# Windowed attention and a routed expert layer on one core: logits in transposed groups, opening products, routing in three steps, scatters without order

## The chip, the core and the metric

The kernel runs on one core of a Trainium2 chip. TensorE (PE) multiplies, VectorE (DVE) and ScalarE (ACT) work on tiles, GpSimd (POOL) builds constants and issues the indirect DMAs, SyncE (SP) and ACT issue the plain ones. All five have queues of their own and wait for each other by semaphores. The metric is the device time of one launch in microseconds: the median of three runs. Beside it there is one profiled execution, from which every duration in this document is read.

## What is computed

Two stages follow each other.

The first is attention in chunks, for 4 batches, 8 heads, 768 tokens and 64 dimensions a head. A chunk of 32 queries sees 8 memory keys, 16 keys to its left, its own 32 and 8 to its right. The outputs of the 8 heads side by side are a token's row x of 512 numbers.

```
scores = scale * q_c @ concat(mem_k, k_ctx).T
a = softmax(scores)
out[:, :, c_start:c_end] = a @ concat(mem_v, v_ctx)
```

The second is a layer of 8 experts, each token using one of them. A token takes the expert with the largest logit (the first of equals), or, if its local gate is at least 0.5, the expert of the token before it in its batch. Its output is weighted with the softmax of the logits at the chosen expert.

```
fresh_e = int(np.argmax(logits[b, s]))
e = fresh_e if s == 0 or local_gate[b, s] < 0.5 else prev_e
h = np.maximum(x[b, s] @ w1[e], 0.0)
out[b, s] = p[e] * (h @ w2[e])
```

All data are float32. A product in float32 shows as two passes in the trace, each with a weight load, so that the counts of products there are twice those of the code. A transpose on TensorE shows as one.

## The kernel before

**Attention.** The 3072 tokens are 32 blocks of 96 tokens, 8 to a batch. `load` (L103) fetches a block's q, k and v, three blocks ahead; q and k are issued by SP, v by ACT. `scores` (L176) makes 8 products, keys by queries, for the two halves of the dimensions' partitions alternately, and ACT turns them into weights with three exps (L188), with the mask as bias. `values` (L191) makes 8 products into one PSUM tile `o_ps`; v carries a column of ones, so that the sum of the weights comes out as the 65th column, and DVE takes its reciprocal (L198) and multiplies (L200) into the token rows `x`. `logits` (L237) turns the block's 96x512 rows by four transposes (L240), ACT copies them to SBUF (L242), and four accumulated products (L245) take the turned tokens as weights and the 9 gate columns (8 experts and the local gate) as the moving operand. DVE copies the 96x9 result (L246).

**Routing.** After the eighth block of a batch `route` (L248) runs once. DVE finds the largest logit and the index of the first, and codes place and expert in one number for tokens that choose anew. Eight products (L273) lay these codes out along one row, four to a PSUM tile, and a running maximum (L277) carries the last choice forward. The expert is cut out of the code by two passes (L279, L280), a one-hot row for each expert is made (L282), and a running sum (L284), carried over batches in `count`, gives each token its rank in its expert. Eight products (L291) bring the row numbers back to the tokens. DVE works out the softmax weight of the chosen expert (L297 to L311), and POOL writes the rows of the eight blocks to `x_dram` in eight indirect scatters (L314), 4096 rows of room for each expert.

**Experts.** When all rows are written, `experts` (L354) works out a table of tiles of 128 rows of one expert each. For every tile, POOL gathers the rows (L435), SP fetches the expert's two weight matrices of 2 MB each (L439, L441; four buffers), PE transposes the rows (L447) and makes 32 products (L460), ACT applies ReLU (L462), PE makes 8 products with 512 moving columns (L465), ACT applies the token's weight (L467) and POOL scatters the output (L468). 24 tiles always run; up to seven more run under conditions.

**Order.** The kernel is written as dataflow on tiles, and a planner at build time sets the order of each engine's instructions and places the semaphores. It is free to move work that doesn't depend on each other: the profile shows the transposes of one block behind the scores of the next. Buffers are reused in a ring for each name. PSUM has two buffers for scores, one tile for `o_ps`, one for transposed blocks (`tps`, L100) and one that logits and the two products of routing share (`xps`, L101). The planner orders two writes to one tensor: each scatter to `x_dram` waits for the one before it, since it can't know that their rows differ.

At the end of attention the kernel counts the softmax sums that lie in a safe range (L342 to L350); only if one doesn't, the whole computation runs again in a shifted form (L82). With the inputs here it doesn't.

Of the kernel before, what the change touches and what calls it, by code (L numbers as in the profile page):

```python
# [8 lines left out]
F32 = mybir.dt.float32  # L9
# [15 lines left out]
MASKED = -1e30  # L25

# [11 lines left out]
SHIFT = 12  # L38
FAR = 4096
WBUF = 4  # L40
# [12 lines left out]
def kernel(  # L53
# [22 lines left out]
    attention(tc, q, k, v, w_gate, w_local, x_dram, ident, count, kept_i)  # L76
    experts(tc, x_dram, out, ident, count, w1, w2)
# [3 lines left out]
    with tc.If(kept < NT * H):  # L81
        attention(tc, q, k, v, w_gate, w_local, x_dram, ident, count, None)  # L82
        experts(tc, x_dram, out, ident, count, w1, w2)
# [3 lines left out]
def attention(ctx, tc, q, k, v, w_gate, w_local, x_dram, ident, count, kept_i):  # L87
# [12 lines left out]
    tps = ctx.enter_context(tc.tile_pool(name="tps", bufs=1, space=PSUM))  # L100
    xps = ctx.enter_context(tc.tile_pool(name="xps", bufs=1, space=PSUM))  # L101

    def load(n):  # L103
        qt = ld.tile([P, HP, QB], F32, name="qt")
        nc.sync.dma_start(qt, q[n])
        kt = ld.tile([P, HP, P], F32, name="kt")
        nc.sync.dma_start(kt, k[n])
        vt = ld.tile([P, H, VW], F32, name="vt")
        nc.scalar.dma_start(vt, v[n])
        return qt, kt, vt  # L110

# [20 lines left out]
    else:  # L132
# [17 lines left out]
        rinvs = once.tile([QB, NB, 2, HP], F32, name="rinvs")  # L150
# [5 lines left out]
    back = once.tile([QB, E], F32, name="back")  # L156
    nc.gpsimd.iota(back, pattern=[[1, E]], base=-E, channel_multiplier=0, allow_small_or_imprecise_dtypes=True)
    place = once.tile([QB, NQB], F32, name="place")
    nc.gpsimd.iota(place, pattern=[[E * QB, NQB]], base=E, channel_multiplier=E,
# [5 lines left out]
    eidx = once.tile([E, 1], F32, name="eidx")  # L165
    nc.gpsimd.iota(eidx, pattern=[[0, 1]], base=0, channel_multiplier=1, allow_small_or_imprecise_dtypes=True)
# [7 lines left out]
    nc.vector.memset(count, 0.0)  # L174

# [15 lines left out]
    def values(pt, vt, n, x):  # L191
        o_ps = ops.tile([QB, 2, 512], F32, name="o_ps")
        ot = o_ps[:, :, 0:HP * VW].rearrange("p u (a d) -> p u a d", a=HP)
        for u in range(2):
            for a in range(HP):
                nc.tensor.matmul(ot[:, u, a], lhsT=pt[:, u, a], rhs=vt[:, 2 * a + u], start=True, stop=True)  # L196
        rinv = rinvs[:, n]
        nc.vector.reciprocal(rinv, ot[:, :, :, DH])  # L198
        for u in range(2):
            nc.vector.tensor_tensor(  # L200
                x[:, 0:D].rearrange("p (a u d) -> p u a d", u=2, d=DH)[:, u], ot[:, u, :, 0:DH],
                rinv[:, u].rearrange("p (a o) -> p a o", o=1).to_broadcast([QB, HP, DH]), op=ALU.mult)
# [17 lines left out]
    def shifted_values(s_sb, vt, n, x):  # L220
        for u in range(2):
            pt_ps = tps.tile([P, HP, QB], F32, name="pt_ps")
# [4 lines left out]
            o_ps = ops.tile([QB, HP, VW], F32, name="so_ps")  # L227
# [9 lines left out]
    def logits(x, lt):  # L237
        xt_ps = tps.tile([P, DK, QB], F32, name="xt_ps")
        for kk in range(DK):
            nc.tensor.transpose(xt_ps[:, kk], x[:, P * kk:P * kk + P], identity=ident[:QB, :QB])  # L240
        xt = sp.tile([P, DK, QB], F32, name="xt")
        nc.scalar.copy(xt, xt_ps)  # L242
        l_ps = xps.tile([QB, E + 1], F32, name="l_ps", tag="xps")
        for kk in range(DK):
            nc.tensor.matmul(l_ps, lhsT=xt[:, kk], rhs=wg[:, kk], start=(kk == 0), stop=(kk == DK - 1))  # L245
        nc.vector.tensor_copy(lt, l_ps)  # L246

    def route(b, x, lt):  # L248
# [7 lines left out]
        nc.vector.scalar_tensor_tensor(  # L256
            first, below, 0.0, back.rearrange("p (o e) -> p o e", o=1).to_broadcast([QB, NQB, E]),
            ALU.is_equal, ALU.mult)
        code = sm.tile([QB, NQB], F32, name="code")
        nc.vector.tensor_reduce(code, first, axis=AX.X, op=ALU.min)  # L260
        nc.vector.tensor_tensor(code, code, place, op=ALU.add)
        fresh = sm.tile([QB, NQB], F32, name="fresh")
        nc.vector.tensor_scalar(fresh, lt[:, :, E], GATE, None, ALU.is_lt)
        nc.vector.memset(fresh[0:1, 0:1], 1.0)
        nc.vector.tensor_tensor(code, code, fresh, op=ALU.mult)


        line = sm.tile([E, S], F32, name="line", bufs=2)
        for half in range(2):
            c_ps = xps.tile([E, HALF, QB], F32, name="c_ps", tag="xps")  # L270
            for j in range(HALF):
                n = HALF * half + j
                nc.tensor.matmul(c_ps[:, j], lhsT=code[:, n:n + 1].to_broadcast([QB, E]), rhs=ident[:QB, :QB],  # L273
                                 start=True, stop=True)
            nc.vector.tensor_copy(line[:, HQ * half:HQ * half + HQ], c_ps.rearrange("p j n -> p (j n)"))
        run = sm.tile([E, S], F32, name="run", bufs=2)
        nc.vector.tensor_tensor_scan(run, line, line, 0.0, ALU.max, ALU.max)  # L277
        expert = sm.tile([E, S], I32, name="expert", bufs=2)
        nc.vector.tensor_copy(expert, run)  # L279
        nc.vector.tensor_scalar(expert, expert, E - 1, None, ALU.bitwise_and)  # L280
        onehot = sm.tile([E, S], F32, name="onehot", bufs=2)
        nc.vector.tensor_scalar(onehot, expert, eidx, None, ALU.is_equal)  # L282
        rank = sm.tile([E, S], F32, name="rank", bufs=2)
        nc.vector.tensor_tensor_scan(rank, onehot, onehot, count, ALU.add, ALU.max)  # L284
        nc.vector.tensor_copy(count, rank[:, S - 1:S])


        nc.vector.scalar_tensor_tensor(rank, rank, region, onehot, ALU.add, ALU.mult)  # L288
# [233 lines left out]
```

## Time and profile before

| what | value |
|---|---|
| median of three runs | 768.44 us (767.79 to 768.86) |
| profiled execution | 768.29 us, span 766.6 us |
| TensorE products busy | 647.7 us (84%), 3810 instructions |
| weight loads busy | 520.7 us (68%) |
| VectorE, ScalarE, GpSimd busy | 103.6, 106.4, 85.3 us |
| DMA | 156.92 MB, mean 205 GB/s |
| mean granted TensorE clock | 0.976 |

The profile gives times from the span's start. "PE" is TensorE's products, "PEld" its weight loads, which overlap the products. A line of a group of instructions has the source line, the engine, the operation, output and inputs by their names, the shape, the count, then the busy time, the mean duration of one in ns, and the idle time of the engine before them with what ended it. The duration of one product holds its way through the array, so that the distance of two products is less than it; distances are taken from the length of an unbroken row of products and its count. In the line of slices a digit is the busy share of a fortieth of the span, in tenths. "PEclk" is the granted clock of TensorE as a share of full speed, as the throttle's records have it.

### The profile page before, as it was taken

What the parts mean: (1) busy time and instruction counts of PE and PEld (TensorE: products, weight loads), DVE (VectorE), ACT (ScalarE), POOL (GpSimd) and SP (SyncE); (2) the same over time, 40 slices, a digit from 0 to 9 for tenths busy, and PEclk for the clock granted to TensorE, in tenths of its full rate; (3) what the DMA queues carried; (4) which work ended last, traced back from release to release, by engine and by line L of the source; (5) the groups of instructions that cost most, each with busy time, mean ns of one, the idle gap of its engine ahead of it and who ended that gap; (6) DMA issues with size and microseconds to landing.
All of it is one profiled execution on the core that took longest, in us unless ns stands there. A gap on an engine that the chain in (4) does not pass through costs nothing.

```text
span 766.6 us, 9247 instructions
## 1 busy us (share of the span) xinstructions
PE 647.7 (84%) x3810; PEld 520.7 (68%) x3810; DVE 103.6 (14%) x332; ACT 106.4 (14%) x214; POOL 85.3 (11%) x106
## 2 busy tenths in 40 slices
PE   6999999699998410499999999999999999966680
PEld 6999999599898310476776786687677677654460
DVE  1112412511431620100000000000000000000000
ACT  2212222022222000010110111111011111100000
POOL 1000021020002023011211111111121110011100
PEclk9999999999999999999999999999999999988985
DMA  7333335254312014999998888888888888600000
GB/s 239 100 105 100 115 106 156 69 142 135 91 49 58 4 41 140 425 428 422 427 360 313 314 322 313 323 311 319 343 295 335 325 297 332 242 26 28 28 3 5
DMA packets 29078, 156.92 MB, mean 205 GB/s; under 512 B 5021, under 2 KB 9117, under 8 KB 22112
## 3 DMA queue, kind: packets, MB, share of 16 engines
q1 hardware_dynamic: 16992, 127.93, 44.5%
q0 software_dynamic: 6368, 19.72, 7.2%
q10 hardware_dynamic: 5664, 8.54, 4.2%
q8 instruction: 34, 0.56, 0.3%
q14 instruction: 20, 0.16, 0.1%
HBM read 143.57 MB, written 13.39 MB: 205 GB/s over the span
## 4 chain that ended last, share of the span: by engine, by line
issue 32%; PE 31%; DMA 31%; DVE 3%; POOL 0%; POOLq 0%; ACT 0%; SPq 0%; ACTq 0%; DVEq 0%
DMA out_dram<-y,to 24%; PE o_ps L196 11%; PE s_ps L183 8%; PE l_ps L245 5%; PE xt_ps L240 4%; DMA x_dram<-x,row 3%; DMA xs<-x_dram,rows 3%; PE c_ps L273 1%; PE r_ps L291 1%; DMA kt<-in_k_dram 1%; DVE x L200 1%; DVE rank L284 0%; DVE run L277 0%; POOL out_dram L468 0%; DVE rank L288 0%
## 5 line engine op out<-in xcount | busy, mean ns | idle before, releaser
L460 PEld LDWEIGHTS h_ps<-xt,w_sb 128*128 128x128 f32 x1728 | 203.4, 198 | 15.6 <-DVE xt L449 8.2
L460 PE MATMUL h_ps<-xt,w_sb 128*128 128x128 f32 x1728 | 205.9, 282 | 5.8 <-DVE xt L449 5.0
L465 PE MATMUL y_ps<-w_sb,ht 128*128 128x512 f32 x432 | 189.9, 592 | 0.0
L465 PEld LDWEIGHTS y_ps<-w_sb,ht 128*128 128x128 f32 x432 | 80.0, 190 | 90.4 <-issue 90.4
L196 PE MATMUL o_ps<-vt,pt 128*96 128x65 f32 x512 | 93.6, 364 | 0.0
L196 PEld LDWEIGHTS o_ps<-vt,pt 128*96 128x96 f32 x512 | 88.6, 280 | 1.7 <-issue 1.0
L183 PE MATMUL s_ps<-qt,kt 64*128 64x96 f32 x512 | 72.1, 435 | 6.8 <-DMA kt<-in_k_dram 6.3
L447 PE MATMUL g_ps<-ident,xs 128*128 128x128 f32 x108 | 18.0, 313 | 63.8 <-DMA xs<-x_dram,rows 63.8
L183 PEld LDWEIGHTS s_ps<-qt,kt 64*128 64x128 f32 x512 | 61.8, 323 | 12.4 <-issue 8.5
L468 POOL DMA_INDIRECT out_dram<-y,to x27 | 27.1, 1002 | 386.1 <-ACT y L467 364.3
L462 ACT ACTIVATE ht<-h_ps 128x512 f32<-128x512 f32 x54 | 32.2, 597 | 269.6 <-PE h_ps L460 269.6
L447 PEld LDWEIGHTS g_ps<-ident,xs 128*128 128x128 f32 x108 | 14.4, 161 | 72.7 <-issue 63.2
L314 POOL DMA_INDIRECT x_dram<-x,row x32 | 29.5, 923 | 265.0 <-DVE x L311 189.4
L451 DVE TENSOR_TENSOR to<-xs,past 128x1 int32<-128x1 f32 x27 | 4.3, 160 | 371.0 <-DMA out_dram<-y,to 226.6
L245 PEld LDWEIGHTS l_ps<-wg,xt 128*96 128x96 f32 x256 | 44.7, 279 | 1.4 <-ACT xt L242 0.9
L245 PE MATMUL l_ps<-wg,xt 128*96 128x9 f32 x256 | 44.6, 304 | 0.6 <-ACT xt L242 0.6
L467 ACT ACTIVATE y<-y_ps,xs 128x512 f32<-128x512 f32 x27 | 18.6, 687 | 170.7 <-PE y_ps L465 164.3
L188 ACT ACTIVATE pt<-s_ps,mask_mid 128x256 f32<-128x256 f32 x72 | 29.4, 471 | 68.5 <-PE s_ps L183 35.8
L240 PE MATMUL xt_ps<-ident,x 96*128 96x96 f32 x128 | 29.4, 380 | 5.4 <-DVE x L200 5.3
L242 ACT COPY xt<-xt_ps 128x384 f32<-128x384 f32 x32 | 15.3, 478 | 92.0 <-PE xt_ps L240 88.2
L435 POOL DMA_INDIRECT xs<-x_dram,rows x27 | 26.1, 967 | 11.1 <-issue 8.0
L240 PEld LDWEIGHTS xt_ps<-ident,x 96*128 96x128 f32 x128 | 19.9, 219 | 10.9 <-issue 10.2
(103 smaller groups left out, 166.4 us busy)
## 6 DMA issues: line engine op xcount, KB each, us to landing
w_sb<-in_w_dram SPq DMA_DIRECT2D x54, 2048.0 KB, 8.9
vt<-in_v_dram ACTq DMA_DIRECT2D x32, 260.0 KB, 2.7
kt<-in_k_dram SPq DMA_DIRECT2D x32, 256.0 KB, 3.4
qt<-in_q_dram SPq DMA_DIRECT2D x32, 192.0 KB, 2.6
x_dram<-x,row POOLq DMA_INDIRECT x32, 3.1
xs<-x_dram,rows POOLq DMA_INDIRECT x27, 7.4
out_dram<-y,to POOLq DMA_INDIRECT x27, 8.0
wg<-in_w_gate_dram ACTq DMA_DIRECT2D x1, 16.0 KB, 6.1
```

The lines of the kernel that those rows point to most:

```text
L183: nc.tensor.matmul(st[:, u, a], lhsT=kt[h, a], rhs=qt[h, a], start=True, stop=True)
L188: nc.scalar.activation(pt[:, :, :, c], st[:, :, :, c], ACT.Exp, bias=m[:, g:g + 1], scale=SCALE)
L196: nc.tensor.matmul(ot[:, u, a], lhsT=pt[:, u, a], rhs=vt[:, 2 * a + u], start=True, stop=True)
L240: nc.tensor.transpose(xt_ps[:, kk], x[:, P * kk:P * kk + P], identity=ident[:QB, :QB])
L245: nc.tensor.matmul(l_ps, lhsT=xt[:, kk], rhs=wg[:, kk], start=(kk == 0), stop=(kk == DK - 1))
L314: nc.gpsimd.indirect_dma_start(out=x_dram[:, :], out_offset=bass.IndirectOffsetOnAxis(ap=row[:, n:n + 1], axis=0), in_=x[:, n].bitcast(I32 ...
L435: nc.gpsimd.indirect_dma_start(out=xs.bitcast(I32), out_offset=None, in_=x_dram[:, :], in_offset=bass.IndirectOffsetOnAxis(ap=rows[:, i:i ...
L447: nc.tensor.transpose(g_ps[:, kk], xs[:, P * kk:P * kk + P], identity=ident)
L460: nc.tensor.matmul(h_ps[:, m], lhsT=w1_sb[:, kk, P * (g + m):P * (g + m) + P], rhs=xt[:, kk], start=(kk == 0), stop=(kk == DK - 1))
L462: nc.scalar.activation(ht[:, g:g + 4], h_ps, ACT.Relu)
L465: nc.tensor.matmul(y_ps, lhsT=ht[:, m], rhs=w2_sb[:, m], start=(m == 0), stop=(m == FK - 1))
L468: nc.gpsimd.indirect_dma_start(out=out, out_offset=bass.IndirectOffsetOnAxis(ap=to, axis=0), in_=y, in_offset=None, bounds_check=NT - 1, o ...
```

## The change

Five things are changed; the rest of the kernel stays.

1. **Zero products.** Before the first loads are used, four products of a 128x512 tile of zeros are issued into the PSUM buffer of `o_ps`. Their result is not read.
2. **Logits of four blocks at once.** The turned tokens of four blocks are gathered in one tile. Four accumulated products take the 9 gate columns as weights and 384 tokens as moving operand. The 9x384 result is copied by ACT and turned back by four small transposes, and DVE clamps it to plus or minus 1e30 while copying it.
3. **Routing in three steps.** `route_picks`, `route_ranks` and `route_rows` are issued one block apart, and transposing a block (`turned`) comes one block after its `values`. The choice is carried as one-hot columns: a product brings 8 columns "chosen anew here" and 8 columns "keeps the last" to the expert's rows, and a scan `state * keep + new` in two halves gives the one-hot rows at once. The code of place and expert, the running maximum and the integer passes fall away.
4. **Scatters without order.** The scatters to `x_dram` are declared independent of each other, and every gather gets a dependence on all 32 of them instead.
5. **PSUM.** `o_ps` becomes two tiles, one for each half of the heads, with a reciprocal each. The transposed blocks, logits, picks and ranks share two buffers.

The integer table of experts is also limited to 7 (L423). The shifted form is changed in the same places.

```diff
+WARM = 4
...
-    tps = ctx.enter_context(tc.tile_pool(name="tps", bufs=1, space=PSUM))
-    xps = ctx.enter_context(tc.tile_pool(name="xps", bufs=1, space=PSUM))
+    xps = ctx.enter_context(tc.tile_pool(name="xps", bufs=2, space=PSUM))
...
+        zeros = once.tile([P, 512], F32, name="zeros")
+        nc.vector.memset(zeros, 0.0)
+        z_ps = ops.tile([P, 512], F32, name="z_ps", tag="o_ps0")
+        for _ in range(WARM):
+            nc.tensor.matmul(z_ps, lhsT=zeros[:, 0:P], rhs=zeros, start=True, stop=True)
...
+    picks = [once.tile([QB, NQB, KEEP + E], F32, name=f"picks{i}") for i in range(2)]
...
     def values(pt, vt, n, x):
...
         for u in range(2):
+            o_ps = ops.tile([QB, HP, VW], F32, name="o_ps", tag=f"o_ps{u}")
             for a in range(HP):
-                nc.tensor.matmul(ot[:, u, a], lhsT=pt[:, u, a], rhs=vt[:, 2 * a + u], start=True, stop=True)
...
+                nc.tensor.matmul(o_ps[:, a], lhsT=pt[:, u, a], rhs=vt[:, 2 * a + u], start=True, stop=True)
+            rinv = rinvs[:, n, u]
+            nc.vector.reciprocal(rinv, o_ps[:, :, DH:VW])
...
-    def logits(x, lt):
-        xt_ps = tps.tile([P, DK, QB], F32, name="xt_ps")
+    def turned(x, xt):
+        xt_ps = xps.tile([P, DK, QB], F32, name="xt_ps", tag="xps")
         for kk in range(DK):
             nc.tensor.transpose(xt_ps[:, kk], x[:, P * kk:P * kk + P], identity=ident[:QB, :QB])
...
+    def logits(xt, lt):
+        lt_ps = xps.tile([E + 1, HALF, QB], F32, name="lt_ps", tag="xps")
         for kk in range(DK):
-            nc.tensor.matmul(l_ps, lhsT=xt[:, kk], rhs=wg[:, kk], start=(kk == 0), stop=(kk == DK - 1))
-        nc.vector.tensor_copy(lt, l_ps)
...
+            nc.tensor.matmul(lt_ps, lhsT=wg[:, kk], rhs=xt[:, kk], start=(kk == 0), stop=(kk == DK - 1))
+        lt_sb = sp.tile([E + 1, HALF, QB], F32, name="lt_sb")
+        nc.scalar.copy(lt_sb, lt_ps)
+        l_ps = xps.tile([QB, HALF, E + 1], F32, name="l_ps", tag="xps")
+        for j in range(HALF):
+            nc.tensor.transpose(l_ps[:, j], lt_sb[:, j], identity=ident[:E + 1, :E + 1])
...
+        nc.vector.tensor_scalar(lt, l_ps, BIG, -BIG, ALU.min, ALU.max)
...
+    def route_ranks(b):
...
+            c_ps = xps.tile([KEEP + E, HALF, QB], F32, name="c_ps", tag="xps")
             for j in range(HALF):
...
+                nc.tensor.matmul(c_ps[:, j], lhsT=picks[b % 2][:, HALF * half + j], rhs=ident[:QB, :QB],
                                  start=True, stop=True)
...
+            stays = sm.tile([E, HQ], F32, name="stays", bufs=2)
+            nc.scalar.copy(stays, c_ps[KEEP:KEEP + E].rearrange("p j n -> p (j n)"))
+            nc.vector.tensor_tensor_scan(
+                onehot[:, HQ * half:HQ * half + HQ], stays, c_ps[0:E].rearrange("p j n -> p (j n)"),
+                onehot[:, HQ - 1:HQ] if half else 0.0, ALU.mult, ALU.add)
...
         for n in range(NQB):
-            nc.gpsimd.indirect_dma_start(
+            ins = nc.gpsimd.indirect_dma_start(
                 out=x_dram[:, :], out_offset=bass.IndirectOffsetOnAxis(ap=row[:, n:n + 1], axis=0),
...
+            tc.declare_no_dep(ins, group=group, reason="rows are unique")
+            tc.add_to_no_dep_group(group, ins)
+            scatters.append(ins)
...
+    for n in range(NB + 3):
+        if n < NB:
...
+            ahead = begin(n + 1) if n + 1 < NB else None
+            make_values(*begun, n, xs[b][:, j])
...
+        if 0 <= n - 1 < NB:
...
+            turned(xs[b][:, j], xts[(n - 1) // HALF][:, :, j % HALF])
+            if j % HALF == HALF - 1:
+                logits(xts.pop((n - 1) // HALF), lts[b][:, j - HALF + 1:j + 1])
+            if j == NQB - 1:
+                belows[b] = route_picks(b, lts.pop(b))
+        if 0 <= n - 2 < NB and (n - 2) % NQB == NQB - 1:
...
+            ranks[b] = route_ranks(b)
+        if 0 <= n - 3 < NB and (n - 3) % NQB == NQB - 1:
...
+            route_rows(b, xs.pop(b), belows.pop(b), ranks.pop(b))
...
+        for s in scatters:
+            tc.add_manual_dep(ins, s.name, mybir.DependencyInfo(
+                mybir.DependencyClass.Sync, mybir.DependencyReason.DATA), reason="rows written")
```

More of the change, by code (lines that the diff above doesn't have):

```diff
@@ L255, in route @@
         first = sm.tile([QB, NQB, E], F32, name="first")
[L256 to L259, printed above, removed]
+        nc.vector.scalar_tensor_tensor(first, below, 0.0, back.to_broadcast([QB, NQB, E]), ALU.is_equal, ALU.mult)
+        code = sm.tile([QB, NQB, 1], F32, name="code")
         nc.vector.tensor_reduce(code, first, axis=AX.X, op=ALU.min)
-        nc.vector.tensor_tensor(code, code, place, op=ALU.add)
@@ L350, in attention, with experts @@
         nc.vector.tensor_copy(kept_i, k_ps)
+    return scatters
 @with_exitstack
-def experts(ctx, tc, x_dram, out, ident, count, w1, w2):
+def experts(ctx, tc, x_dram, scatters, out, ident, count, w1, w2):
     nc = tc.nc
```

100 lines of the change are left out of this document (46 added, 54 removed).

## The prediction, before the changed kernel was run

> **What bounds the kernel now.** I read the slices of the span first, for the stages, then sums by window. Columns: window and length, busy time of PE, weight load, DVE, ACT and POOL, granted clock, DMA share, GB/s.
>
> ```profile
> PE   6999999699998410499999999999999999966680
> PEclk9999999999999999999999999999999999988985
> ...
> 34.15:62.09 27.94, 27.94 (x178) 26.18 (x177) 4.29 (x16) 6.61 (x16) 0.00 (x0) 1.00 0.35 105
> 138.80:145.00 6.20, 0.00 (x0) 0.00 (x0) 5.99 (x8) 0.00 (x0) 0.00 (x0) 1.00 0.22 74
> 254.80:273.20 18.40, 6.56 (x38) 5.42 (x38) 12.08 (x40) 0.26 (x1) 0.01 (x1) 1.00 0.00 0
> 273.20:300.80 27.60, 0.00 (x0) 0.00 (x0) 2.28 (x11) 0.00 (x0) 7.34 (x8) 1.00 0.19 57
> 300.80:320.90 20.10, 4.13 (x16) 3.02 (x17) 2.30 (x5) 0.00 (x0) 3.83 (x4) 1.00 0.98 396
> 320.90:766.60 445.70, 401.33 (x2254) 292.62 (x2252) 19.64 (x49) 50.80 (x81) 49.34 (x50) 0.96 0.70 267
> ```
>
> Attention ends with the last logits at 254.8 us; then 18.4 us of routing for the last batch, 27.6 us of scatters with PE idle, 20.1 us of gathers and weight loads, and 445.7 us of experts. The change touches the first three only. In attention the bound is TensorE: 27.94 us busy of 27.94 in a stretch of four blocks, 6.985 us a block, with ACT and DVE under a quarter busy.
>
> The question is what that busy PE costs. The product groups of the attention stage (busy us, mean ns of one), then weight loads of the same 128 columns in two stretches of an expert tile, one at granted clock 0.50 and one at 1.00:
>
> ```profile
> L196 PE MATMUL o_ps<-vt,pt 128*96 128x65 f32 x512 | 93.6, 364 | 0.0
> L183 PEld LDWEIGHTS s_ps<-qt,kt 64*128 64x128 f32 x512 | 61.8, 323 | 12.4 <-issue 8.5 <-ACT pt L188 0.8
> L245 PE MATMUL l_ps<-wg,xt 128*96 128x9 f32 x256 | 44.6, 304 | 0.6 <-ACT xt L242 0.6
> L240 PE MATMUL xt_ps<-ident,x 96*128 96x96 f32 x128 | 29.4, 380 | 5.4 <-DVE x L200 5.3
> L273 PE MATMUL c_ps<-ident,code 96*8 96x96 f32 x64 | 11.6, 363 | 2.3 <-DVE code L265 1.7 <-DVE line L275 0.6
> L291 PE MATMUL r_ps<-ones,rank 8*96 8x1 f32 x64 | 10.8, 293 | 13.6 <-DVE tiles_i L383 7.4 <-DVE rank L288 6.3
> ...
> L460 PEld LDWEIGHTS h_ps<-xt,w_sb 128*128 128x128 f32 x20 | 4.3, 330 | 1.2 <-DVE xt L449 1.2
> L460 PEld LDWEIGHTS h_ps<-xt,w_sb 128*128 128x128 f32 x41 | 4.7, 192 | 0.0
> ...
> L465 PE MATMUL y_ps<-w_sb,ht 128*128 128x512 f32 x432 | 189.9, 592 | 0.0
> ```
>
> A load of 128 columns takes 330 ns at clock 0.50 and 192 at 1.00. In attention it takes 323 over all 512 of them. So attention runs at half clock from end to end. The PEclk row says 9 there; I take it that it shows full speed until the first change is recorded, and believe the durations. The expert products start the same way and recover:
>
> ```profile
> 320.94 8.83 PE L460 MATMUL h_ps<-xt,w_sb 128*128 128x128 f32 x64
> 336.48 7.31 PE L460 MATMUL h_ps<-xt,w_sb 128*128 128x128 f32 x64
> ...
> 666.79 7.03 PE L465 MATMUL y_ps<-w_sb,ht 128*128 128x512 f32 x16
> 679.80 1.09 PE L447 MATMUL g_ps<-ident,xs 128*128 128x128 f32 x4 [5.98 <-DMA xs<-x_dram,rows]
> ...
> 672.00:676.00 4.00, 1.82 (x5) 0.52 (x3) 0.00 (x0) 0.69 (x1) 0.97 (x1) 1.00 0.01 2
> 676.00:680.00 4.00, 0.20 (x1) 0.23 (x2) 0.16 (x1) 0.00 (x0) 0.98 (x1) 0.89 0.37 115
> 680.00:684.00 4.00, 3.22 (x15) 2.82 (x15) 0.69 (x1) 0.00 (x0) 0.00 (x0) 0.50 0.02 4
> 684.00:688.00 4.00, 4.00 (x29) 4.00 (x29) 0.00 (x0) 0.37 (x1) 0.00 (x0) 0.76 0.00 0
> ```
>
> Two facts follow. Raising: at 320.94 the 64 products took 8.83 us against 7.31, which is some 15 at 215 ns (4.3/20) before the rest at 114 (7.31/64): 3.3 us of dense products. The 0.76 puts the later rise at 684+0.24*4/0.5 = 685.9. Falling: products end at 673.8, and the 0.89 puts the fall at 680-0.11*4/0.5 = 679.1, after 5.3 us of silence. The stretch 672 to 676, busy 1.82 us of 4, kept its clock. So a product stream that is broken, but not silent for microseconds, keeps a clock that dense products raised; and attention's stream, busy throughout, has never raised it. What it lacks is moving columns: 8 logits products a block move 9 columns each behind loads of 96.
>
> **The change, part by part.** All sums go against the profiled execution, 768.29 us (span 766.6 and 1.7 around it), 0.15 below the median of the three timed runs, 768.44.
>
> *Zero products.* Four, in two passes each, of 128x512, between a DVE memset and the first scores. A pass of 512 at full clock takes (7.03-0.592)/15 = 0.429 us (its group row gives 592 ns for one). Eight passes last 6.9 us at half clock. The rise needs about 3.3 us of dense products, so it comes inside them. The DVE begins at 0.89; the nearest row for the memset is
>
> ```profile
> 0.89 0.06 DVE L174 MEMSET count<- 8x1 f32 x1 [0.89 <-PEq L514]
> 5.76 2.03 PE L183 MATMUL s_ps<-qt,kt 64*128 64x96 f32 x16 [5.76 <-DMA kt<-in_k_dram]
> 0.00:20.00 20.00, 13.66 (x92) 12.59 (x92) 2.95 (x20) 5.37 (x11) 2.57 (x20) 1.00 0.70 229
> ```
>
> one of 8x1; for 512 columns I allow 0.3 to 0.7. So they run from 1.5 to between 6.6 (raised after 3.4 us) and 8.4 (never): the first scores, which could start at 5.76, lose 0.8 to 2.6 us; taken 7.5.
>
> *Logits.* The nine gate columns become the weights and 384 tokens move: 8 passes of 384*0.429/512 = 0.322 us, 2.57 us for four blocks at full clock, plus four small transposes bounded by L240 (29.4/32 = 0.92 a block at half clock, so at most 0.46): some 0.75 a block. The old ones cost 44.6/32 = 1.39 at half clock, so 0.70 at full. By itself the edit is worth nothing: +0.05 a block at full clock, up to +0.10 at half (3 us in all).
>
> *The clock, on all other products.* 6.985 halves to 3.49, and 3.54 with the new logits. That is the lower end: 113 us for 32 blocks. The upper end: no row shows LDWEIGHTS and MATMUL pairs at full clock closer than L460's 114 ns, and scores would need 63 (half of 2.03/16). With 36 products and block transposes and one small transpose at 114 and two passes of 0.322, a block is 4.9 us, 156 in all, and the time 682. The expert transposes and products halved with the clock, so I stay near the lower end: 3.75, 120 us. The Trainium skill (TensorE: Matmul & The Clock Gate, "Back-to-back issue gap") speaks for a floor in between: some 81 ns for each pair of load and product of 128 columns, sustained, which would hold the scores alone above 63; as an estimate 3.54 + 16*0.018 = 3.83 a block, and the time 649. No row here shows that spacing. Routing's products on PE, (11.6+10.8)/4 = 5.6 a batch, halve to 2.8; three batches lie inside the loop, 8.4.
>
> *What else must keep up in 3.75 us.*
>
> ```profile
> L188 ACT ACTIVATE pt<-s_ps,mask_mid 128x256 f32<-128x256 f32 x72 | 29.4, 471 | 68.5 <-PE s_ps L183 35.8 <-PE o_ps L196 32.7
> L242 ACT COPY xt<-xt_ps 128x384 f32<-128x384 f32 x32 | 15.3, 478 | 92.0 <-PE xt_ps L240 88.2 <-PE l_ps L245 3.9
> L200 DVE TENSOR_TENSOR x<-o_ps,rinvs 96x256 f32<-96x256 f32 x64 | 24.6, 413 | 0.9
> L198 DVE RECIPROCAL rinvs<-o_ps 96x8 f32<-96x8 f32 x32 | 6.5, 204 | 52.1 <-PE o_ps L196 52.1
> L284 DVE TENSOR_TENSOR_SCAN rank<-onehot,count 8x768 f32<-8x768 f32 x4 | 7.2, 1802 | 0.1
> L277 DVE TENSOR_TENSOR_SCAN run<-line 8x768 f32<-8x768 f32 x4 | 6.9, 1732 | 0.1
> ```
>
> ACT: three exps and a copy, 1.9 us, and 0.3 for the new copies. DVE: two reciprocals now and two products, 1.23, and about 1.1 a block of routing (some twenty operations near 0.2 and 4.8 us of ranks, over eight blocks). DMA: 0.35 of 27.94 us is 2.4 us of the 16 engines a block, 65%; the first 20 us show 0.70 at 229 GB/s, so it fits. None is the bound on average, but the DVE comes in bursts: the step of ranks holds two half scans, the rank scan and its product, about 4.8 us during which the next block's o_ps waits. The old routing stalled PE 6.2 us in one place (138.8 to 145.0). I put 10 us of stalls for the stage; bounds 0 (the three steps hide all) and 25 (four times 6.2).
>
> *End of attention.* 7.5 + 120 + 8.4 + 3 for filling and draining (an exp of 1.2, DVE 1.2, a copy) + 10 = 149, against 254.8: minus 106.
>
> *Last batch.* Logits come four blocks at once, and through a copy and transposes: 2.5 us later. In return the 18.4 us lose the separate scan of L277 (1.7) and the three passes over 768 elements behind it (none under L242's 0.48 for 384, taken 2.2 in all), less 0.2 for a new small operation: about 3.7. Sum: minus 1.
>
> *Scatters.* They wait for each other now; weights wait for the last:
>
> ```profile
> 273.19 0.92 POOL L314 DMA_INDIRECT x_dram<-x,row  x1 [25.04 <-DVE x L311]
> 276.77 0.92 POOL L314 DMA_INDIRECT x_dram<-x,row  x1 [2.66 <-DMA x_dram<-x,row]
> ...
> 296.81 0.92 POOL L314 DMA_INDIRECT x_dram<-x,row  x1 [2.83 <-DMA x_dram<-x,row]
> 300.49 0.35 SPq L439 DMA_DIRECT2D w_sb<-in_w_dram  x1
> ...
> 300.84 0.97 POOL L435 DMA_INDIRECT xs<-x_dram,rows  x1 [3.11 <-DMA x_dram<-x,row]
> 302.11 0.96 POOL L435 DMA_INDIRECT xs<-x_dram,rows  x1 [0.30 <-issue]
> ```
>
> Without the waits they follow like the gathers, 1.27 us apart: 7*1.27 and 3.7 for the last to land is 12.6, against 27.3: minus 14.7. Behind a waiting gather on POOL stand only later gathers and output scatters; the 32 added dependences cost nothing there, and every gather needs the last scatter already. The weights still wait for it, and the experts' 465.8 us are unchanged.
>
> Sum: 768.3 - 106 - 1 - 14.7 = 646.6; I say **646**.
>
> **Rivals.** (a) The clock is raised and then lost in gaps: at the start, where values wait for the first exp, or at a DVE burst. For: 1.82 us busy of 4 is the emptiest stretch seen to hold, and attention's products move columns only part of their time. Against: nothing shorter than 5 us of silence lowered it. Half the stage slow: 646 + 53 = 699. The Trainium skill (same page, "A second HAM failure mode: psum-queue depth-cycling") has a kernel whose clock swings because PE idles briefly between groups; no run here shows that yet.
> (b) The clock never helps: zeros do not count as work, or the stage drops at once. Then zero products cost 2.6, logits 3, and the stall of 6.2 goes: 768.3 - 0.6 - 1 - 14.7 = 752. For: attention never raised it by itself; against: the expert rows.
> (c) Slower: at half clock, the transposed blocks, both logits forms, picks and ranks share two PSUM buffers where the transposed blocks had their own. If the products wait each time for a reader queued behind an exp on ACT (1.2+0.48, twice per four blocks), that is 3.4*8 = 27 us: 752 + 27 = 779. It is slower from 0.5 us a block on. Against: the buffers' readers are far from busy.
> (d) The scatters stay serial after all: 646 + 14.7 = 661, inside the forecast's own range. The gathers on the same queue speak against it.
>
> **How the numbers follow.** Forecast 0.70 (with d), own range 620 to 685 from stalls 0 to 25 and a block of 3.54 to 4.3; (a) 0.12; (b) 0.13; (c) 0.05. The range 612 to 715 holds nearly all of the forecast and of (a). A difference of 0.2%, 1.5 us, is about what this kernel's timing tells from none. Faster: 0.70 + 0.12 + 0.13 less 0.02 where (b) loses its gain; same 0.02; slower 0.05.
>
> **What would show it.** The 128-column loads of scores near 190 ns, not 323, from the zero products on; a block near 3.7 us; no fall of the granted clock before the last batch's routing; last logits near 150; eight scatters within 13 us. Loads that stay at 323 make (b) true, a mean in between (a); a PE with idle time before each transposed block at full clock would put the loss on readers or DVE and the time above 685.

## The result and the profile after

The changed kernel takes 681.07 us, median of four runs (670.88 to 683.1), against 768.65 before. It is faster by some 88 us, where 122 were forecast. The ratio of 0.879, 95% interval 0.868 to 0.890, goes by the two timed runs that count as fast, 670.88 and 680.79 us; the slower profiled execution, 683.1 us with a span of 681.4, had nearly the mean granted clock of the second of them (0.873 against 0.876).

The slices of the changed kernel, then its sums by window, from the last logits on and for two stretches of attention (window and length, busy time of PE, weight load, DVE, ACT, POOL, granted clock, DMA share, GB/s):

```profile
PE   8999899999830499999999999999999999696580
PEclk9996676676655599999999999999999999887895
...
24.56:39.66 15.10, 15.10 (x158) 12.05 (x157) 4.90 (x17) 7.17 (x17) 0.00 (x0) 1.00 0.65 195
72.01:92.49 20.48, 19.85 (x113) 15.69 (x114) 4.60 (x17) 5.42 (x13) 0.00 (x0) 0.50 0.44 121
186.80:202.10 15.30, 6.58 (x38) 6.09 (x38) 9.19 (x36) 1.19 (x3) 0.00 (x0) 0.54 0.00 0
202.10:214.90 12.80, 0.00 (x0) 0.00 (x0) 2.67 (x12) 0.00 (x0) 7.58 (x8) 0.50 0.42 123
214.90:235.80 20.90, 4.20 (x17) 3.09 (x18) 2.30 (x5) 0.00 (x0) 3.82 (x4) 0.50 0.95 389
235.80:681.40 445.60, 401.61 (x2253) 292.89 (x2252) 19.63 (x49) 50.79 (x81) 49.34 (x50) 0.95 0.70 267
```

The PEclk row has fives, sixes and sevens in attention now: from the first recorded change on, the granted clock swings between 1.00 and 0.50. The forecast had it at full speed until the last batch. Step by step:

| step | forecast | measured | from |
|---|---|---|---|
| end of the zero products | 7.5 | 7.9 | first scores at 7.95 |
| a block at full clock, with its logits | 3.75 | 3.78 | 15.10 / 4 |
| last logits | 149 + 2.5 | 186.8 | window |
| routing of the last batch after them | 14.7 | 15.3 | window |
| last scatters to first weight load | 12.6 | 12.8 | window |
| first weight load to the end of the span | 466.1 | 466.5 | 681.4 - 214.9 |
| time | 646 | 681 | |

Nearly all of the miss lies in the stage of attention, and there in the clock. Its records give seven falls (54.95, 72.01, 106.14, 123.21, 157.34, 174.41, 188.06) and seven rises (7.16, 65.19, 92.49, 116.39, 143.69, 167.59, 184.65) up to the routing of the last batch. Between 8 us and the last logits 81.9 us are at half clock. At half clock half of the work is done, so these cost 41 us. The forecast for the last logits, 151.5, less the 10 us that it had for stalls, plus the 7.2 us in which TensorE stood (171.56 us busy of 178.80), plus 41, is 190; the other terms were 3 us too high together.

The weight loads of the scores show the same in nanoseconds, first between 9 and 50 us, then between 73 and 90. Then the zero products, the first scores, and two blocks at full clock:

```profile
L193 PEld LDWEIGHTS s_ps<-qt,kt 64*128 64x128 f32 x178 | 11.6, 187 | 2.4 <-issue 1.3
...
L193 PEld LDWEIGHTS s_ps<-qt,kt 64*128 64x128 f32 x46 | 5.3, 324 | 0.7 <-issue 0.7
...
1.54 6.47 PE L120 MATMUL z_ps<-zeros 128*128 128x512 f32 x8 [1.54 <-DVE count L180]
7.95 2.03 PE L193 MATMUL s_ps<-qt,kt 64*128 64x96 f32 x32
11.88 1.14 PE L193 MATMUL s_ps<-qt,kt 64*128 64x96 f32 x16
12.95 1.57 PE L205 MATMUL o_ps<-vt,pt 128*96 128x65 f32 x16
14.36 0.50 PE L248 MATMUL xt_ps<-ident,x 96*128 96x96 f32 x4
14.79 1.14 PE L193 MATMUL s_ps<-qt,kt 64*128 64x96 f32 x16
15.85 1.57 PE L205 MATMUL o_ps<-vt,pt 128*96 128x65 f32 x16
```

187 ns is a load of 128 columns at full clock, 324 at half. From values to values a block takes 2.90 us; its 16 score products stand 67 ns apart ((12.95-11.88)/16), well under the 114 that was the closest distance that the prediction had found in the trace before.

**Where the clock falls and rises.** The distances between all these changes are multiples of 3.413 us: 54.95 to 65.19 is three of them, 72.01 to 92.49 is six. So the clock changes at the ends of the windows of a fixed grid. The windows that end in the first fall, the first rise of the stage, the second fall and the second rise:

```profile
51.53:54.95 3.42, 3.15 (x33) 2.79 (x32) 2.55 (x7) 0.91 (x3) 0.00 (x0) 1.00 0.56 155
61.77:65.18 3.41, 3.41 (x16) 1.74 (x15) 0.00 (x0) 0.02 (x1) 2.75 (x3) 0.50 0.78 234
68.60:72.01 3.41, 2.24 (x28) 1.73 (x26) 0.33 (x3) 0.00 (x0) 1.14 (x2) 1.00 0.88 281
89.08:92.49 3.41, 3.41 (x7) 0.73 (x6) 0.00 (x0) 0.00 (x0) 0.00 (x0) 0.50 0.00 0
```

Both falls come out of windows with PE busy, 3.15 and 2.24 of 3.4 us. What both rises have is few long products: x16 and x7, the logits streams of 384 columns. The first fall holds routing: TensorE brings the ranks back by products with one column (16 of them from 54.02 on), after a wait of 0.27 us for the scan of ranks. The second holds pauses of TensorE, 0.52 us ahead of 71.12 and 1.28 us ahead of 72.64:

```profile
67.21 0.89 PE L205 MATMUL o_ps<-vt,pt 128*96 128x65 f32 x8
68.03 0.35 PE L260 MATMUL l_ps<-ident,lt_sb 9*96 9x9 f32 x4
69.04 0.50 PE L248 MATMUL xt_ps<-ident,x 96*128 96x96 f32 x4
69.12 0.92 POOL L332 DMA_INDIRECT x_dram<-x,row  x1 [0.30 <-issue]
69.75 0.18 DVE L207 RECIPROCAL rinvs<-o_ps 96x4 f32<-96x4 f32 x1 [8.44 <-PE xt_ps L248]
71.86 0.19 DVE L262 TENSOR_SCALAR lt<-l_ps 96x36 f32<-96x36 f32 x1 [1.93 <-PE s_ps L193]
71.97 0.41 DVE L208 TENSOR_TENSOR x<-o_ps,rinvs 96x256 f32<-96x256 f32 x1
72.33 0.48 ACT L249 COPY xt<-xt_ps 128x384 f32<-128x384 f32 x1 [3.75 <-PE s_ps L193]
72.64 2.80 PE L205 MATMUL o_ps<-vt,pt 128*96 128x65 f32 x16 [1.28 <-DVE rinvs L207]
...
76.06 0.17 DVE L330 COPY x<-token 96x8 f32<-96x8 f32 x1
```

The experiments were planned with this reading: there are two buffers for a batch's rows `x`; at 71.97 the first block of the third batch is written into the buffer from which the first batch's last scatter was issued at 69.12, and until then DVE stands, and TensorE behind it. The trace doesn't bear it out. Line L208 has two rows a block, and 26 of them come before 71.97: this is the sixth block of the second batch, whose buffer has been in use for five blocks. The instruction that does wait for the first batch's eight scatters is the copy of the tokens at 76.06, and no idle time stands before it. What the rows show is that DVE and ACT take up results of TensorE late: the first values end at 68.10 and their reciprocal starts at 69.75, the turned logits end at 68.38 and their copy starts at 71.86, the transposes end at 69.54 and their copy starts at 72.33. The same comes at 119 to 123.2, and at 170 to 173.9 in the last batch, behind which no batch needs a buffer. What delays them is open; the trace of this execution also lacks 315 of 3808 records of landed transfers, where the traces of the experiments lack three at most.

The first theory for the experiments was this: the clock rises after a window filled with moving columns, and falls after one with too few of them.

### The profile page after: what moved, and what is told of

Read it like the earlier page. It is cut to its first block, busy times and chain, and to the rows that moved or that the text cites. A ratio compares the mean times of both kernels' runs of the same rounds, so it can differ in the third digit from the quotient of the medians.

```text
span 681.4 us, 8954 instructions
## 1 busy us (share of the span) xinstructions
PE 590.4 (87%) x3658; PEld 438.0 (64%) x3658; DVE 97.0 (14%) x329; ACT 113.5 (17%) x230; POOL 86.0 (13%) x106
## 4 chain that ended last, share of the span: by engine, by line
issue 36%; DMA 31%; PE 25%; DVE 4%; POOL 1%; ACT 1%; POOLq 0%; another core or an unknown queue 0%; DVEq 0%
DMA out_dram<-y,to 27%; PE o_ps L205 9%; PE s_ps L193 6%; PE lt_ps L255 5%; DMA xs<-x_dram,rows 3%; PE xt_ps L248 2%; PE r_ps L309 1%; DVE rank L299 1%; DVE onehot L295 1%; POOL x_dram L332 1%; PE z_ps L120 1%; PE c_ps L291 1%; DMA x_dram<-x,row 0%; DVE x L208 0%; PE l_ps L260 0%
## 5 line engine op out<-in xcount | busy, mean ns | idle before, releaser
L205 PE MATMUL o_ps<-vt,pt 128*96 128x65 f32 x512 | 65.8, 290 | 4.6 <-DVE rinvs L207 3.4
L205 PEld LDWEIGHTS o_ps<-vt,pt 128*96 128x96 f32 x512 | 59.5, 202 | 9.9 <-issue 7.0
L193 PE MATMUL s_ps<-qt,kt 64*128 64x96 f32 x512 | 52.4, 329 | 1.3 <-issue 1.3
L193 PEld LDWEIGHTS s_ps<-qt,kt 64*128 64x128 f32 x512 | 43.2, 227 | 12.1 <-issue 9.4
L255 PE MATMUL lt_ps<-xt,wg 128*9 128x384 f32 x64 | 31.8, 661 | 0.6 <-ACT xt L249 0.6
L208 DVE TENSOR_TENSOR x<-o_ps,rinvs 96x256 f32<-96x256 f32 x64 | 26.7, 417 | 1.4
L491 DVE COPY xt<-g_ps 128x512 f32<-128x512 f32 x27 | 17.7, 687 | 61.3 <-PE g_ps L489 61.3
L249 ACT COPY xt<-xt_ps 128x384 f32<-128x384 f32 x32 | 15.3, 478 | 58.8 <-PE xt_ps L248 46.6
L207 DVE RECIPROCAL rinvs<-o_ps 96x4 f32<-96x4 f32 x64 | 10.9, 174 | 93.6 <-PE o_ps L205 75.6
```

Source lines behind the costliest of these rows:

```text
L193: nc.tensor.matmul(st[:, u, a], lhsT=kt[h, a], rhs=qt[h, a], start=True, stop=True)
L205: nc.tensor.matmul(o_ps[:, a], lhsT=pt[:, u, a], rhs=vt[:, 2 * a + u], start=True, stop=True)
L208: nc.vector.tensor_tensor(x[:, 0:D].rearrange("p (a u d) -> p u a d", u=2, d=DH)[:, u], o_ps[:, :, 0:DH], rinv.to_broadcast([QB, HP, DH]), ...
L255: nc.tensor.matmul(lt_ps, lhsT=wg[:, kk], rhs=xt[:, kk], start=(kk == 0), stop=(kk == DK - 1))
```

## The experiments

**Three x buffers.**

```diff
-    xp = ctx.enter_context(tc.tile_pool(name="xp", bufs=2))
+    xp = ctx.enter_context(tc.tile_pool(name="xp", bufs=3))
```

> The changed kernel with three buffers for the token rows x instead of two; nothing else. Theory M (moving columns): the clock is looked at in a free-running grid of 3.41 us, rises after a window in which products move columns for most of it, and falls after one in which they do so for less than about a third; the falls at 72.0 and 123.2 us come from a pause of the products, because the first block of a batch waits for the scatters of the batch two before to leave its x buffer. Then the pause and both falls vanish, two slow stretches of 20.5 us run at full clock and two pauses of about 2 us go: minus 20 to 25, near 657. Rival T (traffic or time): the scatters' traffic or a limit of its own lowers the clock; the falls stay at the same places behind the scatters, and only the pauses go: near 677.

649.04 us (647.22 to 653.04), ratio to before 0.846 (0.843 to 0.850), less than the 657 of theory M. The pauses are gone, and so are the falls behind them. Three falls are left in the stage, all in routing, and each is followed by 6.8 us at half clock instead of 10.2: 20.5 us in all instead of 81.9. The slices, the window of the first fall and the last scatters:

```profile
PEclk9997998978557999999999999999999999797795
...
53.18:56.59 3.41, 3.41 (x39) 3.16 (x38) 1.30 (x7) 1.14 (x3) 0.00 (x0) 1.00 0.30 78
56.59:63.42 6.83, 6.83 (x32) 4.05 (x31) 1.31 (x6) 1.02 (x3) 4.51 (x5) 0.50 0.70 209
167.60:180.40 12.80, 0.00 (x0) 0.00 (x0) 2.66 (x12) 0.00 (x0) 7.59 (x8) 0.50 0.42 123
```

The last scatters take as long as in the changed kernel, and the falls behind the scatters are gone all the same, so rival T falls. The 61 us less at half clock are 31 us of the 32 us that lie between the medians of the two kernels. That the third buffer removes the pauses is not shown. The changed kernel was not run again beside the experiments; only the kernel before was, at 768.33 us here and 768.65 there. TensorE, ACT, GpSimd and SP have their instructions in the same order in both kernels, and DVE but for the copies of the tokens. In two more pairs of runs below, in which the kernel with two buffers has no such late results either, the third buffer is worth nothing: 651.09 us with two and 652.09 with three (64 columns), 666.58 and 665.26 (no zero products). The clock falls at 56.59 after a window in which PE was busy all the time, so PE's busy time isn't what decides.

**64 columns for the ranks, alone and with three x buffers.**

```diff
+WIDE = 64
...
-    ones = once.tile([E, 1], F32, name="ones")
+    ones = once.tile([E, WIDE], F32, name="ones")
...
-        r_ps = xps.tile([QB, NQB], F32, name="r_ps", tag="xps")
+        r_ps = xps.tile([QB, NQB, WIDE], F32, name="r_ps", tag="xps")
...
```

> The changed kernel with the ones that bring the ranks back 64 columns wide instead of 1, so that these 8 products move 64 columns each behind the same weight loads of 96; one column of the result is used. Theory M: the windows ending at 54.9, 106.1 and 157.3 us hold these products and move columns for 0.2 to 0.3 of their time; 64 columns add about 0.17, enough to hold the clock. Three slow stretches of 10.2 us go: minus 10 to 15, near 668; the falls behind the wait for x stay. Rival I (idle): the clock falls because TensorE waits for the DVE's long scans, whatever the products move; no fall vanishes, 681.

> Both: three x buffers and the 64 columns. Theory M: no fall is left before the routing of the last batch; the stage's 82 us at half clock take 41 less, near 642, which is what the prediction's sum had without its clock losses. Rivals T and I: at least one kind of fall stays, 660 or more.

651.09 (650.25 to 655.68) and 652.09 us (651.45 to 652.49). What theory M expected of the 64 columns failed in both: the clock fell in all three routings again (at 56.87, 94.42 and 135.38 alone; at 54.77, 95.73 and 136.69 together). Alone, the fall of its first routing, with the products of 64 columns in the window:

```profile
53.46:56.87 3.41, 3.41 (x40) 3.14 (x39) 1.64 (x9) 1.29 (x4) 0.14 (x1) 1.00 0.33 78
...
53.29 1.57 PE L310 MATMUL r_ps<-ones,rank 8*96 8x64 f32 x16
```

These products have only 8 rows. Columns that move over 8 of 128 rows don't hold the clock, and the theory had to say rows. That the kernel with two x buffers gained 30 us all the same has another cause: none of the late results of the changed kernel is there, and so none of the three falls behind them. The planner gave DVE another order here, TensorE the same. This kernel does wait for an x buffer:

```profile
71.42 0.17 DVE L331 COPY x<-token 96x8 f32<-96x8 f32 x1 [1.90 <-DMA x_dram<-x,row]
```

It costs TensorE 0.79 us, and no fall follows.

**Without zero products.**

```diff
-WARM = 4
+WARM = 0
```

> The changed kernel without the four zero products. Theory M: the first blocks run at half clock until the first logits of four blocks, 8 passes of 384 columns in a row, fill a window and raise it: four blocks lose 2.45 us each and one logits stream up to 2.5, and the start gains 2.2 because the first scores needn't wait: plus 5 to 12, near 689. Rival Z: only the zero products can raise the clock of this stage; without them it stays at half, near 745.

> The changed kernel with three x buffers and without the zero products, to be compared with the one with three x buffers (649.0), whose clock falls only in routing. Theory M: half clock until a logits stream covers a whole window, the first or the second (25 to 40 us): plus 8 to 15, 657 to 664. Rival N: the zero products cost at the start what they save; within 3 us of 649.

With two x buffers 666.58 us (662.84 to 668.5), less than the changed kernel, where theory M had 689 and rival Z 745: a miss of both. The first rise came at 40.20, with the first logits stream (36.54 to 41.08), as theory M had it, and the first batch's scatters began 12.1 us later (72.5 against 60.4). But no late results and no falls behind them came, though there are two x buffers and the instructions have the order of the changed kernel but for one copy of tokens; so it won more than it lost. With three x buffers neither kernel has the pauses, and the price shows: 665.26 us (663.22 to 667.64), just above the range of theory M, against 649.04: 16 us. So the zero products do raise the clock, and the logits streams do it without them, later. The window of the rise without zero products:

```profile
36.79:40.20 3.41, 3.41 (x6) 0.69 (x5) 0.00 (x0) 0.00 (x0) 0.00 (x0) 1.00 0.00 0
```

(The 1.00 is what the row shows ahead of the first recorded change; the six products of 384 columns in 3.41 us are at half clock.)

**The old logits in the changed kernel.**

```diff
...
-            nc.tensor.matmul(lt_ps, lhsT=wg[:, kk], rhs=xt[:, kk], start=(kk == 0), stop=(kk == DK - 1))
...
+            nc.tensor.matmul(l_ps, lhsT=xt[:, kk], rhs=wg[:, kk], start=(kk == 0), stop=(kk == DK - 1))
...
```

> The changed kernel with the logits of before: per block, turned tokens as weights, 9 moving columns; zero products, three steps and scatters as changed. Theory M (the clock rises after a grid window in which products move 128-row columns for about three quarters of it, holds above about a third, falls below): the zero products raise it, the first routing loses it near 50 us as in the changed kernel, and nothing raises it again, since only the logits streams filled a window; 23 blocks at 6.98 us follow: last logits near 215 us against 187, and a time of 700 to 715. Rival L: the new logits matter only by their own time, which at half clock is that of the old ones; within 5 us of 681, with rises where they were.

713.44 us (712.09 to 715.26), last logits at 216.7: both as theory M had them. The clock fell at 57.42 and never rose again in the stage:

```profile
PEclk9996555555555559999999999999999999988895
...
57.42:216.70 159.28, 158.03 (x954) 145.53 (x953) 43.43 (x165) 35.54 (x85) 22.19 (x24) 0.50 0.35 102
```

So the turned logits, which the prediction priced at nothing, are worth 32 us against the changed kernel's median. Two things are in this. Behind the zero products they are the only ones of the stage that raise the clock. And the old ones cost more themselves: from values to values a block takes 4.06 us at full clock and 7.39 at half here, against 3.67 ((3*2.90 + 5.97)/4, the fourth block with the logits) and some 6.6 with the new ones (5.3 for three of four blocks, 10.3 for the one with the logits).

**Two parts alone in the kernel before.** Zero products:

```diff
+        zeros = once.tile([P, 512], F32, name="zeros")
+        nc.vector.memset(zeros, 0.0)
+        z_ps = ops.tile([P, 2, 512], F32, name="o_ps")
+        for _ in range(4):
+            nc.tensor.matmul(z_ps[:, 0], lhsT=zeros[:, 0:P], rhs=zeros, start=True, stop=True)
...
```

> The kernel before with the four zero products and nothing else. Theory M: raised by 8 us, attention's stream holds it (it moves columns for about 0.45 of its time), the first routing near 40 us loses it for good: 9 blocks at 3.5 instead of 7.0, less 2 us at the start, near 740. Rival Z: a stream that never raised the clock doesn't hold it either; lost within the first blocks, 768 to 771. Rival H: it holds to the end of attention, below 690.

732.66 us (730.71 to 734.11), 7 less than theory M had, and far from both rivals. The old stream holds a raised clock for fifteen windows and loses it in routing at 58.15 for good, later than expected. Scatters without order:

```diff
...
+            tc.declare_no_dep(ins, group=group, reason="rows are unique")
+            tc.add_to_no_dep_group(group, ins)
...
```

> The kernel before with the scatters declared independent and the gathers made dependent on all of them; nothing else. From the prediction's row: eight scatters of the last batch in 12.6 us instead of 27.3, all of it on the path: 753 to 755. Rival D: the scatters stay serial or their traffic makes each land later: 764 or more.

747.84 us (747.25 to 749.14), below the expected 753: 20.5 less than before, where the prediction's row gives 14.7. Two windows tell why:

```profile
138.80:145.00 6.20, 6.20 (x44) 5.68 (x43) 5.50 (x9) 1.68 (x4) 0.00 (x0) 1.00 0.39 117
...
266.70:279.20 12.50, 0.00 (x0) 0.00 (x0) 2.33 (x11) 0.00 (x0) 7.35 (x8) 1.00 0.43 126
```

The last eight scatters take 12.5 us instead of 27.3, as forecast. But between 138.8 and 145.0, where TensorE stood still before, it is busy throughout, and the last logits start at 248.0 instead of 254.4. Before, the third batch's first write to its x buffer, which waits for the first batch's scatters, stood behind the rank scans in DVE's order, at 144.82, though the last of these scatters had landed at 129.81; now it stands ahead of the scans, at 131.35, and TensorE has products of the next blocks to make while DVE scans. That the planner had put it late because the serial scatters held the buffer longer is argued, not shown.

**Zero products in routing, with three x buffers** (1, 2 and 3 of them, in the PSUM buffer of the ranks, ahead of these):

```diff
...
-        r_ps = xps.tile([QB, NQB], F32, name="r_ps", tag="xps")
+        r_ps = xps.tile([P, 512], F32, name="r_ps", tag="xps")
+        for _ in range(0 if shifted else HOLD):
+            nc.tensor.matmul(r_ps, lhsT=zeros[:, 0:P], rhs=zeros, start=True, stop=True)
+        r_ps = r_ps[:QB, 0:NQB]
```

> Three x buffers, and one zero product of 128x512 (two passes, 0.86 us at full clock) ahead of the products that bring the ranks back, in their PSUM buffer. Theory M: the windows that lose the clock in routing move 128-row columns for 0.2 of their time; 0.86 us adds 0.25 to one window or a part of it to each of two, so some of the three falls go. Of the 20.5 us at half clock some 10 are lost; at most 2.6 are paid: 640 to 649. Rival W (the falls come from something in routing other than too few moving columns): all three stay, 650 to 652.

> The same with two zero products, 1.7 us in four passes. Theory M: 0.5 of a window, or 0.25 in each of two: no fall before the last batch; about 10 won, at most 5.1 paid, much of it in TensorE's own waits for the rank scan: 639 to 645. Rival W: 651 to 654.

> The same with three zero products, 2.6 us in six passes. Theory M: no fall, but nothing more to win and up to 0.86 more paid for each batch than with two: 640 to 648, 0 to 2.6 above it. Rival W: 653 to 657.

648.93 us (645.89 to 652.27), 650.33 (647.98 to 654.07) and 654.14 (644.47 to 660.2). The first lies at the upper end of its range, the others above theirs; none is clearly below three x buffers alone. In the profiled executions with one and with two, two falls of the three in the stage are left (54.78 and 133.29; 90.87 and 135.25), so what theory M had for two, no fall before the last batch, did not come. But the profiled execution with three of them is the one of all these whose clock held through the whole stage:

```profile
PEclk9999999997557999999999999999999999797795
...
8.00:150.30 142.30, 139.16 (x1357) 108.00 (x1353) 62.19 (x213) 60.57 (x145) 22.21 (x24) 1.00 0.60 184
```

Last logits at 150.3 us, time 644.47: near the prediction's 151.5 and 646, with the condition that it had named and the changed kernel didn't meet. The other three executions of this kernel took 651.8, 656.5 and 660.2 us at mean granted clocks of 0.925, 0.920 and 0.913 against 0.938; they lost the clock somewhere, and where wasn't traced. With zero products in routing the phase of the grid may still decide; that is only argued.

**All windows together.** Counted over the windows of 3.413 us of thirteen profiled executions (before, after and the eleven experiments) that lie between 2 us and the last logits. The moving columns are taken, for every product, as its columns times 0.84 ns (0.429 us for 512; twice that at half clock) ahead of its end, as a share of the window; in the last two measures times its rows over 128. The last number of a line is how many windows lie where the two ranges overlap.

```
341 windows at full clock        the clock fell (27)   it held          overlap
time in which TensorE is busy    0.51 to 1.00          0.69 to 1.00     337
columns                          0.15 to 0.58          0.27 to 1.16      74
columns x rows/128               0.08 to 0.38          0.27 to 0.87      29
the same, transposes counted     0.12 to 0.38          0.40 to 0.87       0

340 windows at half clock        the clock rose (35)   it stayed        overlap
time in which TensorE is busy    0.88 to 1.00          0    to 1.00     310
columns                          0.87 to 1.18          0    to 1.23      94
columns x rows/128               0.68 to 1.11          0    to 0.72       4
the same, transposes counted     0.82 to 1.11          0    to 0.73       0
```

The transposes are left out of the second and third measure. Some shares come out above 1, since the ends of products are modelled. With rows and transposes counted two thresholds separate all 681 windows: a share of some 0.4 to hold and of some 0.75 to rise. Counted from the products' starts, the falls go up to 0.36 and the holds begin at 0.37, and the rises begin where the others end, at 0.77; so the thresholds are known to some 0.05. They are fitted to these windows, and no run tests them on others. Of the 27 falls 24 lie in windows with the products that bring the ranks back, and the other three are the changed kernel's pauses. All 35 rises lie in windows with zero products or a logits stream. Attention's other products come to 0.45 to 0.63 in the mean of longer stretches, in both forms of the logits. That fits a stream that never raises the clock and mostly holds it. The number of columns of the weights doesn't count: the logits streams have 9 and raise it.

## Why the prediction was right and wrong

**The bound and the reading of the clock: right.** That attention before ran at half clock from end to end, though the clock's row showed full speed, is confirmed by the runs: with loads of 187 ns instead of 324 a block without logits takes 2.90 us instead of 5.32 in the changed kernel.

**The terms at full clock: right.** A block at 3.78 us against 3.75, routing of the last batch 15.3 against 14.7, scatters 12.8 against 12.6, experts 466.5 against 466.1. The upper bound of 4.9 us a block, for pairs of load and product that can't follow closer than 114 ns, is refuted by 67 ns. The prediction's floor in between didn't hold for the scores either: the some 81 ns that the Trainium skill (TensorE: Matmul & The Clock Gate, "Back-to-back issue gap") gives are for 128 moving columns. Here 96 move behind loads of 128, in products of half the rows that alternate between the halves. Values, with 65 moving columns, stand at 88 ns ((14.36 - 12.95)/16, with transposes starting at 14.36).

**Stalls of 10 us: the step that failed.** The stalls themselves were smaller, 7.2 us. But the prediction priced a stall at its own length, and what costs is the clock that is lost: the forecast's condition, "no fall of the granted clock before the last batch's routing", wasn't met, and rival (a) happened, "lost in gaps: at the start, where values wait for the first exp, or at a DVE burst". It was given 0.12. Of its places the start was wrong. The step of ranks was the right place, but not as a gap: TensorE waited 0.27 us there, and its windows lost the clock by products that move one column over 8 rows. The pauses of 1.2 to 1.8 us behind the scatters were in neither list, and what makes them is open. Rival (a)'s price, half the stage, was near: 81.9 us slow of 179.

**"A product stream that is broken, but not silent for microseconds, keeps a clock": wrong.** The windows that fell had PE busy for 1.7 to 3.4 us of 3.4. The observation behind it, 1.82 us busy of 4 without a fall, was dense products of 512 columns for nearly half a window: by the share above that is about 0.44 of the window up to 675.71, over the threshold. The prediction read silence where it should have read columns. The Trainium skill (the same page, "A second HAM failure mode: psum-queue depth-cycling") warned of a clock that swings with short idle spells between groups; the traces agree that it swings, thirteen changes in the stage, but the row of the fall at 56.59 with three x buffers shows no idle spell at all.

**Logits at nothing: mis-sized.** The new ones cost what was forecast, 0.77 us a block at full clock ((5.97 - 2.90)/4) against 0.75. The old ones were put at 0.70, the busy time of their products halved; in the changed kernel they lengthen a block by 1.16 us (4.06 - 2.90). And the new ones raise the clock, which the sum had nothing for: 713 without them.

**Zero products: right.** They raise the clock at 7.16 and are worth 16 us where nothing else confuses the comparison.

**Scatters: right at the end of the kernel, mis-sized as a whole.** 14.7 forecast, 20.5 measured alone: 6.4 more come from the stall in the middle of the stage, which is gone.

**The time.** 681 lies in the range and in the forecast's own range of 620 to 685, but not for the forecast's reason, so that this is luck: the 41 us of lost clock are in no term of the sum. The sum of the other terms was near, as the execution that kept its clock shows (644.47, with three x buffers and more zero products).

## What to carry to other kernels

A stage that keeps TensorE busy can still run at half clock all the time; compare the weight loads of one width in different stages before believing the row of the clock. Once a stream sits between holding and raising, a pause costs not its length but the slow stretch up to the next dense stream: behind a pause of 1.67 us came 20.5 us at half clock. Before a wait is put down to a buffer, find the instruction that waits for it, and count which block it belongs to; and try a remedy in more than one arrangement, for the third buffer came with 32 us in one pair of kernels and with nothing in two. Last, serial scatters that seem to matter only at the end cost 6 us in the middle too.

## What the hardware showed that was not expected

In these thirteen traces the clock of TensorE follows the columns that its products move, weighted with their rows and with transposes counted, in a fixed grid of 3.413 us: it falls below a share of about 0.4 and rises above about 0.75. Products of 8 rows give next to nothing, and the width of the weights has no effect. Between the two it stays as it is, for fifteen windows in the kernel before with zero products and for good in the kernel before. And the same program can land on either side: with three zero products in routing four executions spread from 644.5 to 660.2 us, where those of the kernel before lie within 767.9 and 770.4.
